# Keeping the transposed x in DRAM scratch and loading it per segment, with the gate moved into the FFN and one weight piece fewer streamed

## The chip, the cores and the metric

The kernel runs on one core of a Trainium2 chip. The metric is the device time of one execution in microseconds (us), as the median of several runs. TensorE, VectorE, ScalarE, GpSimd and SyncE are called PE, DVE, ACT, POOL and SP in the profile; PEld is a weight load of TensorE.

## The reference

Two branches see the same 2048 tokens of 640 numbers. Branch a is attention with a memory that recurs over 64 segments of 32 tokens; branch b is a gated FFN; a gate per token mixes them.

```python
g = sigmoid((x * gate_w).sum(-1, keepdims=True))
# a: 64 segments in order, 32 heads of 192; mem is 8 rows
for s in range(64):
    h = concat([mem, x[:, 32*s:32*s+32]])          # 40 rows
    q, k, v = h @ Wq, h @ Wk, h @ Wv               # 640 -> 32 x 192 each
    o = softmax(mask(q @ k.T * 192**-0.5)) @ v @ Wo
    mem = o[:, :8]; outs.append(o[:, 8:])
# b: 640 -> 1536 -> 640
b = (gelu(x @ w_gate) * (x @ w_up)) @ w_down
return g * a + (1 - g) * b                         # bf16, 2048 x 640
```

Wq, Wk, Wv and Wo are 31.5 MB together. They do not fit into SBUF, the core's working memory, and each segment needs all of them, one segment after the other.

## The kernel before

The host code lays out the program with a small scheduler: every operation names the regions that it reads and writes, and waits follow from that. The weights are cut into 84 pieces: 60 of Q, K and V (384 KB, 3072 bytes on each partition) and 24 of Wo (320 KB). What fits stays resident in SBUF; the others are streamed in every segment through a ring of five slots, spread evenly over the segment.

```python
B_RING = int(opts.get("ring", 5))
res_cap = total - wsA_total - wsB_total - ring_bytes
...
while True:                      # smallest number of streamed pieces that fits
    streamed = set()
    for k in range(nstream): ... # evenly over the time of a segment
    if tot_bytes - sum(piece_size(order[i]) for i in streamed) <= res_cap:
        break
    nstream += 1
...
def issue_ring(seg, upto):       # SP loads the next piece into the slot of five pieces ago
    slot = stream_counter[0] % B_RING
    S_.add("sp", lambda e, ...: e.dma_start(piece_view(key, ring_off[slot]), piece_src(key)),
           writes=[r_ring[slot]], dma_sem="ring%d" % slot)
```

A slot is therefore refilled only when TensorE has read it. With this layout 24 pieces are streamed (15 of Q, K, V and 9 of Wo).

First the FFN runs over all tokens and stores b in DRAM. Then the q and k of the last 8 tokens of each segment ("left", because 40 rows are 32 + 8) are computed for all segments and stored. Then come the 64 segments. Every fourth one (a group of 128 tokens) has extra work, in an order of tokens that puts the left ones last, so that rows are moved by two transfers:

```python
def perm_dma(dst, src, reads, writes, sem, watch=False):
    for i in range(2):
        S_.add(AUXQ, lambda e, i=i: e.dma_start(dst(i), src(i)), ...)   # AUXQ is ScalarE's queue
# q == 1: rows of x of the next group into rowb       (perm_dma)
# q == 3: 5 transposes of x, an eviction, 5 gate matmuls; rows of b into rowb (perm_dma)
# q == 0: mix a and b, store the output               (perm_dma)
# every segment: two GpSimd copies of x from the group's Hx into Hb
```

## Time and profile before

The median is 2167.22 us (2161.96 to 2176.56, 3 runs). From the time line, the FFN runs to 181 us, the left phase from 181 to 291 us, and the first segment then waits until 321 us for its left data. The segments follow until the end.

The page's line of engines, and the granted clock, DMA share and rate in 40 slices of the span, for the kernel before:

```profile
PE 1836.7 (85%) x40326; PEld 1154.9 (53%) x40326; DVE 1231.5 (57%) x3952; ACT 618.8 (29%) x1480; POOL 274.1 (13%) x1210
...
DMA  9203579999999999999999999999999999999998
GB/s 366 103 13 89 149 220 341 328 321 337 322 325 316 310 326 329 313 327 311 329 328 314 324 315 332 323 307 316 334 319 333 320 325 306 328 327 328 322 321 273
```

A 9 means that the DMA engines were busy 90% or more of the slice. The segments (slice 6 on, counting from 0) are 9 throughout at 306 to 341 GB/s, apart from the last slice. TensorE is busy 85%.

The windows view over 1400 us of segments gives, in order, the length, the busy time of PE, PEld, DVE, ACT and POOL with the number of instructions, then the clock, the DMA share and the rate:

```profile
500.00:1900.00 1400.00, 1188.97 (x29558) 779.79 (x29555) 878.30 (x2916) 414.44 (x1036) 204.73 (x906) 0.98 0.96 322
```

The waits view of TensorE over the same window names who waited, for what, us in total, times, longest:

```profile
PE ps L872 <- DMA arena<-in_A_Wq_dram: 58.9, 99, 1.9
PE ps L1021 <- DVE arena L1008: 27.8, 78, 0.5
PE ps L992 <- DVE arena L978: 27.6, 73, 0.7
PE ps L1021 <- DMA arena<-in_A_Wo_dram: 24.6, 46, 3.0
PE ps L899 <- DMA arena<-in_A_Wv_dram: 24.0, 41, 1.8
...
PE ps L872 <- DMA arena<-in_A_Wk_dram: 8.0, 12, 1.5
```

All waits for weight pieces come to 120 us here, 2.5 us a segment, more than all others together.

The period of a segment is read from the eviction of the new memory, once per segment on ScalarE. Its line in the view of one source line:

```profile
L1068 ACT ACTIVATE arena<-ps x63: 204/204/205, 353.1 to 2130.9; 128x40 bf16<-128x40 f32 x63
```

63 evictions from 353.1 to 2130.9 us are 62 periods of 28.67 us. A period comes from one profiled execution. The times of one kernel differ by 0.2 to 0.6% from their median, in e1 and e7 by up to 0.8%. So a difference of 0.1 to 0.2 us between two periods means nothing.

ScalarE's queue also issues the permuted transfers. This is the view of their line: duration of the issue (minimum, median, maximum, in ns) and the number.

```profile
L640 ACTq DMA_DIRECT2D arena<-in_A_x_dram x32: 647/684/1298, 0.8 to 1968.0; - x32
L640 ACTq DMA_DIRECT2D arena<-ffn_b_scratch x32: 626/638/662, 420.3 to 2143.7; - x32
L640 ACTq DMA_DIRECT2D out_dram<-arena x32: 651/653/673, 444.1 to 2163.0; - x32
```

Six such issues a group take 3.9 us of ScalarE's in-order queue.

### The profile page before, as it was taken

How to read it: one execution, taken by the hardware profiler on the slowest of the kernel's cores; microseconds unless marked ns; L12 is line 12 of the kernel's file. 1: busy time of each engine (PE TensorE's matmuls, PEld its weight loads, DVE VectorE, ACT ScalarE, POOL GpSimd, SP SyncE). 2: the span in 40 equal slices, each digit the busy share in tenths (PEclk: the TensorE clock that was granted, in tenths of full speed). 3: DMA queues.
4: the chain of work that ended last, by engine and by line, in shares of the span. 5: the costliest groups of instructions: out<-in, count | busy, mean ns of one | idle time of the engine just before them, and what ended most of it. 6: DMA issues, size and time to landing. Idle time of an engine off the chain costs nothing.

```text
span 2166.5 us, 92005 instructions
## 1 busy us (share of the span) xinstructions
PE 1836.7 (85%) x40326; PEld 1154.9 (53%) x40326; DVE 1231.5 (57%) x3952; ACT 618.8 (29%) x1480; POOL 274.1 (13%) x1210
## 2 busy tenths in 40 slices
PE   7999948888888888888888888888888888888887
PEld 3544425555555555555555555555555555555555
DVE  2222316666656566656666666656666666666665
ACT  2222212333232223332322223322323222323232
POOL 0000001111111111111111111111111111111111
PEclk9999979999999999999999999999999999999999
DMA  9203579999999999999999999999999999999998
GB/s 366 103 13 89 149 220 341 328 321 337 322 325 316 310 326 329 313 327 311 329 328 314 324 315 332 323 307 316 334 319 333 320 325 306 328 327 328 322 321 273
DMA packets 363391, 642.97 MB, mean 297 GB/s; under 512 B 60514, under 2 KB 231786, under 8 KB 362986
## 3 DMA queue, kind: packets, MB, share of 16 engines
q1 hardware_dynamic: 311914, 601.41, 81.6%
q10 hardware_dynamic: 51072, 35.66, 5.7%
q8 instruction: 315, 5.16, 0.9%
q14 instruction: 90, 0.74, 0.1%
HBM read 619.13 MB, written 17.83 MB: 294 GB/s over the span
## 4 chain that ended last, share of the span: by engine, by line
DMA 48%; PE 37%; DVE 9%; ACTq 3%; issue 2%; ACT 2%; SPq 0%; POOL 0%; DVEq 0%; POOLq 0%
DMA arena<-in_A_Wq_dram 19%; DMA arena<-in_A_Wo_dram 13%; DMA arena<-in_A_Wv_dram 10%; PE ps L872 9%; PE ps L1021 7%; PE ps L899 5%; DMA arena<-in_A_Wk_dram 4%; PE ps L804 3%; PE ps L742 2%; ACTq L819 2%; PE ps L739 2%; PE ps L757 2%; PE ps L992 2%; DVE arena L975 2%; DVE arena L1008 1%
## 5 line engine op out<-in xcount | busy, mean ns | idle before, releaser
L872 PE MATMUL ps<-arena 128*32 128x384 bf16 x10240 | 566.8, 331 | 119.9 <-DMA arena<-in_A_Wq_dram 77.6
L1021 PE MATMUL ps<-arena 128*128 128x40 bf16 x15360 | 472.1, 181 | 71.7 <-DVE arena L1008 35.9
L1021 PEld LDWEIGHTS ps<-arena 128*128 128x128 bf16 x15360 | 434.9, 97 | 116.8 <-DVE arena L1008 48.0
L872 PEld LDWEIGHTS ps<-arena 128*32 128x32 bf16 x10240 | 239.6, 96 | 346.5 <-DMA arena<-in_A_Wq_dram 172.1
L876 ACT ACTIVATE arena<-ps 128x384 bf16<-128x384 f32 x512 | 251.4, 491 | 552.2 <-PE ps L872 446.8
L899 PE MATMUL ps<-arena 128*32 128x384 bf16 x6400 | 333.1, 331 | 37.0 <-DMA arena<-in_A_Wv_dram 32.2
L835 POOL COPY arena<-arena 128x96 bf16<-128x96 bf16 x256 | 67.6, 264 | 1645.1 <-PE ps L931 1089.0
L899 PEld LDWEIGHTS ps<-arena 128*32 128x32 bf16 x6400 | 150.5, 97 | 175.6 <-DMA arena<-in_A_Wv_dram 82.0
L882 DVE STREAM_TRANSPOSE arena<-arena 128x384 bf16<-128x384 bf16 x256 | 146.0, 570 | 102.3 <-ACT arena L876 102.3
L975 DVE TENSOR_TENSOR arena<-ps,arena 128x320 bf16<-128x320 bf16 x256 | 125.8, 491 | 125.9 <-PE ps L973 121.9
L1002 ACT ACTIVATE arena<-ps 128x320 bf16<-128x320 f32 x256 | 110.7, 432 | 229.4 <-PE ps L994 229.4
L910 ACT ACTIVATE arena<-ps 128x384 bf16<-128x384 f32 x256 | 125.6, 491 | 161.9 <-PE ps L899 161.9
L839 POOL COPY arena<-arena 64x32 bf16<-64x32 bf16 (+1 forms) x768 | 165.7, 216 | 47.3
L959 DVE TENSOR_REDUCE arena<-ps 104x4 f32<-104x160 f32 x256 | 82.6, 323 | 150.6 <-ACT ps L957 148.6
L992 PE MATMUL ps<-arena 128*128 128x160 bf16 (+1 forms) x768 | 133.7, 264 | 39.6 <-DVE arena L978 38.0
L889 DVE STREAM_TRANSPOSE arena<-arena 64x128 bf16<-64x128 bf16 x512 | 145.5, 284 | 8.1
L957 ACT ACTIVATE ps<-ps 104x160 f32<-104x160 f32 x256 | 74.0, 289 | 233.9 <-DVE ps L947 189.0
L994 PE MATMUL ps<-arena 128*128 128x64 bf16 (+1 forms) x768 | 128.0, 206 | 2.1 <-DMA arena<-in_A_Wv_dram 1.0
L945 DVE TENSOR_REDUCE arena<-ps 104x4 f32<-104x160 f32 x256 | 81.0, 316 | 77.0 <-PE ps L931 77.0
L885 DVE STREAM_TRANSPOSE arena<-arena 128x256 bf16<-128x256 bf16 x256 | 111.4, 435 | 16.1 <-ACT arena L876 16.1
L992 PEld LDWEIGHTS ps<-arena 128*128 128x128 bf16 x768 | 73.9, 99 | 85.5 <-DVE arena L978 60.3
L1006 DVE CAST arena<-ps 64x160 bf16<-64x160 f32 x256 | 80.4, 314 | 52.5 <-PE ps L994 48.4
(79 smaller groups left out, 1719.8 us busy)
## 6 DMA issues: line engine op xcount, KB each, us to landing
arena<-in_A_Wo_dram SPq DMA_DIRECT2D x591, 320.0 KB, 4.9
arena<-in_A_Wq_dram SPq DMA_DIRECT2D x404, 384.0 KB, 5.3
arena<-in_A_Wv_dram SPq DMA_DIRECT2D x335, 384.0 KB, 5.1
arena<-in_A_Wk_dram SPq DMA_DIRECT2D x276, 384.0 KB, 5.3
left_qk_scratch<-arena ACTq DMA_DIRECT2D x16, 768.0 KB, 8.8
arena<-left_qk_scratch ACTq DMA_DIRECT2D x64, 192.0 KB, 4.5
arena<-in_A_x_dram SPq DMA_DIRECT2D x4, 640.0 KB, 15.1
ffn_b_scratch<-arena ACTq DMA_DIRECT2D x16, 160.0 KB, 1.8
```

Source lines behind the costliest of these rows:

```text
L839: S_.add("pool", lambda e, a=a, b=b, lo=lo, hi=hi, sa=sa: e.tensor_copy(out=Ks[lo:hi, a:b, L:R], in_=stg[lo:hi, o, 1, sa:sa + b - a]), rea ...
L872: S_.add("pe", [lambda e, j=j, k=k, gv=gv: e.matmul(ps[32 * j:32 * j + 32, bank, 0:384].rearrange("p (c i) -> p c i", i=32), Hb[hb][:, k, ...
L876: S_.add("act", lambda e: e.activation(out=rows_sb[m], in_=ps[:, bank, 0:384], func=ACTF.Copy), reads=[r_ps[bank]], writes=[r_rows[m]], na ...
L882: S_.add("dve", lambda e: e.transpose(out=Qs[:, :, 0:L], in_=rows_sb[0].rearrange("p (c r) -> p c r", r=L)), reads=[r_rows[0]], writes=[r_ ...
L885: S_.add("dve", lambda e: e.transpose(out=apx(Ks[:, 0, :], [[2 * R, 4], [R, 2], [1, L]]), in_=apx(rows_sb[1], [[96, 4], [64, 2], [1, L]])) ...
L889: S_.add("dve", lambda e, a=a, lo=lo: e.transpose(out=Ks[lo:lo + 64, a:a + 4, 0:L], in_=src[lo:lo + 64, :, 1]), reads=[r_rows[1]], writes= ...
L899: return [lambda e, j=j: e.matmul(ps[32 * j:32 * j + 32, bk, 0:384], lhs, g_[:, 384 * j:384 * (j + 1)], start=(k == 0), stop=(k == KT - 1) ...
L910: S_.add("act", lambda e: e.activation(out=v_sb[o % NVB], in_=ps[:, bank, 0:384], func=ACTF.Copy), reads=[r_ps[bank]], writes=[r_v[o % NVB ...
L975: S_.add("dve", lambda e: e.tensor_tensor(out=PTm, in0=apx(pv[:, 512:616], [[64, 2], [0, 4], [1, R]]), in1=apx(mbd, [[0, 2], [1, 4], [0, R]]),
L992: return [lambda e: e.matmul(full, v[:, e0:e0 + 128], PTm[:, ia:ib], start=True, stop=False, skip_group_check=True), lambda e: e.matmul(pa ...
L994: lambda e: e.matmul(part, vl[:, e0:e0 + 128], PTl[:, ia:ib], start=False, stop=True, skip_group_check=True)]
L1021: fns.append(lambda e, g_=g_, i=i, c=c, n=n, tl=tl, cc=cc, u=u: e.matmul(ps[:, OB, n * R:(n + 1) * R], g_[:, i, n * 128:(n + 1) * 128], u[ ...
```

## The change

The FFN transposes x anyway. The change writes that transposed x to DRAM scratch and loads 40 KB of it for each segment, so that the segments need no transposes, no copies and no second order of tokens. The gate is computed in the FFN, and b is stored already multiplied by 1 - g. The smaller buffers free 1408 bytes per partition; with what was spare before, one more piece can stay resident, and 23 are streamed. The intent is fewer weight bytes in each segment.

```diff
-    wsA["H"] = al(2 * KT * R * 2)
-    wsA["Hx"] = al(KT * 128 * 2)
-    wsA["gcol"] = al(2 * 4 * 4)
+    wsA["H"] = al(2 * KT * L * 2)
+    wsA["Hx"] = al(KT * L * 2)
+    wsA["small"] = al(NG * 4 + 8 + 32 + 16)
 ...
-    xT_sb = ....rearrange("p (k t) -> p k t", t=FB)
+    xT_sb = xT_flat.rearrange("p (s k t) -> p k s t", k=KT, t=L)   # 64-byte runs of 32 tokens
 ...
+    def gate_block(blk):            # 80 matmuls of one column, four column positions
+        ...ps[32*j : 32*j+32] <- xT_sb[:, k, sg, :], gwT[:, k:k+1], tile_position=(0, 32 * j)
-    def x_group_transposes(g, bk): ...
-    def gate_group(g, bk): ...
-    def x_copy(s): ...              # GpSimd
+    def x_load(s):                  # 128 packets of 320 bytes, from ScalarE's queue
+        aux_dma(Hb[nb]..., xts[s], ..., "xl%d" % nb)
+    def xleft_load(g):
+        aux_dma(Hx..., xls[g], ..., "xll")
 # at the end of ffn_transposes(blk):
+        aux_dma(xts[16 segments] <- xT_flat)      # 2048 packets of 320 bytes
 # ffn b evac: scale = 1 - g per row
 # segments: perm_dma (two permuted transfers) becomes aux_dma (one contiguous), no x rows, no mix1
-                    if q == 1 and g + 1 < NG:
-                        perm_dma(... rows(x2, g + 1) ...)
-                    if q == 3 and g + 1 < NG:
-                        x_group_transposes(g + 1, misc_bank())
-                        x_copy(s + 1)
+                        x_load(s + 1)
```

More of the change, by code (lines that the diff above doesn't have):

```diff
@@ L263, in _build @@
     b_scr = nc.dram_tensor("ffn_b_scratch", (S, Dm), BF, kind="Internal").ap()
+    xts = nc.dram_tensor("xt_scratch", (NSEG, 128, KT * L), BF, kind="Internal").ap()
+    xls = nc.dram_tensor("left_xt_scratch", (NG, 128, KT * L), BF, kind="Internal").ap()
     qkl = nc.dram_tensor("left_qk_scratch", (NSEG, 128, NOCT * 2 * LW), BF, kind="Internal").ap()
@@ L273, in _build @@
     wsB = {}
-    wsA["H"] = al(2 * KT * R * 2)
-    wsA["Hx"] = al(KT * 128 * 2)
-    wsA["gcol"] = al(2 * 4 * 4)
-    wsA["gwT"] = al(KT * 2)
+    wsA["H"] = al(2 * KT * L * 2)
+    wsA["Hx"] = al(KT * L * 2)
+    wsA["small"] = al(NG * 4 + 8 + 32 + 16)
     wsA["ident"] = al(128 * 2)
-    wsA["e40"] = al(R * 2)
     wsA["maskm"] = al(R * 2)
-    wsA["mbd"] = al(8)
-    wsA["mle"] = al(32)
     wsA["rowb"] = al(Dm * 2)
@@ L349, in sreg @@
         return Rg("sb", o, o + nbytes, plo, phi)
+    for k, n in (("gcol", 0), ("mbd", 4 * NG), ("mle", 4 * NG + 8), ("gwT", 4 * NG + 40)):
+        wsA_off[k] = wsA_off["small"] + n
     o_H = wsA_off["H"]
-    Hb = [bview(o_H + b * KT * R * 2, KT * R * 2).rearrange("p (k r) -> p k r", r=R) for b in range(2)]
-    r_Hm = [sreg(o_H + b * KT * R * 2, 8) for b in range(2)]
-    r_Hxp = [sreg(o_H + b * KT * R * 2 + 8, KT * R * 2 - 8) for b in range(2)]
+    Hb = [bview(o_H + b * KT * L * 2, KT * L * 2).rearrange("p (k r) -> p k r", r=L) for b in range(2)]
+    r_Hm = [sreg(o_H + b * KT * L * 2, 8) for b in range(2)]
+    r_Hxp = [sreg(o_H + b * KT * L * 2 + 8, KT * L * 2 - 8) for b in range(2)]
     o_Hx = wsA_off["Hx"]
-    Hx = bview(o_Hx, KT * 256).rearrange("p (k t) -> p k t", t=128)
-    r_Hx = sreg(o_Hx, KT * 256)
-    gcol = fview(wsA_off["gcol"], 32)
-    r_gcol = [sreg(wsA_off["gcol"] + 16 * b, 16) for b in range(2)]
+    Hx = bview(o_Hx, KT * L * 2).rearrange("p (k t) -> p k t", t=L)
+    r_Hx = sreg(o_Hx, KT * L * 2)
+    gcol = fview(wsA_off["gcol"], 4 * NG)
+    r_gcol = sreg(wsA_off["gcol"], 4 * NG)
+    gtmp = fview(o_Hx + 256, 32)
+    r_gtmp = sreg(o_Hx + 256, 32)
     gwT = bview(wsA_off["gwT"], KT * 2)
@@ L363, in _build @@
     r_ident = sreg(wsA_off["ident"], 256)
-    e40 = bview(wsA_off["e40"], R * 2)
-    r_e40 = sreg(wsA_off["e40"], R * 2)
+    e40 = ident[:, 0:R]
+    r_e40 = r_ident
     maskm = bview(wsA_off["maskm"], R * 2)
@@ L374, in _build @@
     r_rowb = sreg(wsA_off["rowb"], Dm * 2)
-    r_rowbh = [sreg(wsA_off["rowb"], Dm * 2, 0, 4 * XA), sreg(wsA_off["rowb"], Dm * 2, 4 * XA, 128)]
     Qs = bview(wsB_off["Q"], 12 * R * 2).rearrange("p (s r) -> p s r", r=R)
@@ L408, in _build @@
     r_aT4 = sreg(wsB_off["aT4"], KT * 256)
-    mem0r = bview(wsB_off["aT4"], Dm * 2)
-    r_mem0r = sreg(wsB_off["aT4"], Dm * 2)
-    gwr = bview(wsB_off["p"], 256)
-    r_gwr = sreg(wsB_off["p"], 256)
-    assert wsB_off["p"] >= ffn_off["brow"]
+    mem0r = rowb
+    r_mem0r = r_rowb
+    gwr = bview(o_Hx, 256)
+    r_gwr = sreg(o_Hx, 256)
     wg_sb = bview(ffn_off["wg"], KT * Df * 2).rearrange("p (k f) -> p k f", f=Df)
@@ L422, in _build @@
     r_xr = [sreg(ffn_off["xr"] + b * FA * Dm * 2, FA * Dm * 2) for b in range(2)]
-    xT_sb = bview(ffn_off["xT"], KT * FB * 2).rearrange("p (k t) -> p k t", t=FB)
-    r_xT = [sreg(ffn_off["xT"] + k * FB * 2, FB * 2) for k in range(KT)]
+    xT_flat = bview(ffn_off["xT"], KT * FB * 2)
+    xT_sb = xT_flat.rearrange("p (s k t) -> p k s t", k=KT, t=L)
+    r_xT = [sreg(ffn_off["xT"], KT * FB * 2)]
     gl_sb = [bview(ffn_off["gl"] + b * FB * 2, FB * 2) for b in range(2)]
@@ L434, in _build @@
     o_XL = ffn_base - XLB
-    XL = bview(o_XL, XLB).rearrange("p (k t) -> p k t", t=NL)
+    XL_flat = bview(o_XL, XLB)
+    XL = XL_flat.rearrange("p (g k t) -> p k g t", k=KT, t=L)
     r_XL = sreg(o_XL, XLB)
@@ L609, in _build @@
            reads=[r_ident], writes=[r_ident])
-    S_.add("pool", lambda e: e.memset(e40, 1.0), writes=[r_e40])
-    S_.add("pool", lambda e: e.affine_select(out=e40, in_=e40, pattern=[[-1, R]], compare_op=ALU.is_equal,
-                                             fill=0.0, base=0, channel_multiplier=1),
-           reads=[r_e40], writes=[r_e40])
     def asel(ap, reg, pattern, base, cm, fill):
@@ L630, in _build, with aux_dma @@
         S_.add("dve", lambda e, b=b: e.memset(ps[:, b, :], 0.0), writes=[r_ps[b]])
-    PP = (slice(0, 4 * XA), slice(4 * XA, 128))
-    def rows(ap, g):
-        v = ap[128 * g:128 * g + 128, :].rearrange("(s t) d -> s t d", t=L)
-        return v[:, 0:XA, :], v[:, XA:L, :]
-    def perm_dma(dst, src, reads, writes, sem, watch=False):
-        for i in range(2):
-            S_.add(AUXQ, lambda e, i=i: e.dma_start(dst(i), src(i)), reads=reads, writes=writes[i:i + 1],
-                   dma_sem="%s%d" % (sem, i), watch=watch, name=sem)
+    def aux_dma(dst, src, reads, writes, sem, watch=False):
+        S_.add(AUXQ, lambda e: e.dma_start(dst, src), reads=reads, writes=writes, dma_sem=sem, watch=watch, name=sem)
     def ffn_x_load(blk):
@@ L651, in _build @@
            writes=[r_gwr], dma_sem="gwr")
-    perm_dma(lambda i: rowb[PP[i]], lambda i: rows(x2, 0)[i], [], r_rowbh, "rowb")
     ffn_x_load(0)
@@ L658, in _build @@
     S_.add("sp", lambda e: e.dma_start(wd_sb, w_down.rearrange("(f p) n -> p f n", p=128)), writes=[r_wd], dma_sem="wd")
-    def x_group_transposes(g, bk):
-        pv = psb(bk)
-        S_.add("pe", [lambda e, k=k: e.transpose(pv[:, k * 128:(k + 1) * 128], rowb[:, k * 128:(k + 1) * 128], ident)
-                      for k in range(KT)],
-               reads=[r_rowb, r_ident], writes=[r_ps[bk]], name="xT g%d" % g)
-        S_.add("dve", lambda e: e.tensor_copy(out=Hx, in_=pv[:, 0:KT * 128].rearrange("p (k t) -> p k t", t=128)),
-               reads=[r_ps[bk]], writes=[r_Hx], name="xT evac g%d" % g)
@@ L667, in gate_group @@
-    def gate_group(g, bk):
-        b = g % 2
-        lg = ps[:, bk, 400:401]
-        S_.add("pe", [lambda e, k=k: e.matmul(lg, Hx[:, k, :], gwT[:, k:k + 1], start=(k == 0), stop=(k == KT - 1))
-                      for k in range(KT)],
-               reads=[r_Hx, r_gwT], writes=[r_ps[bk]], name="gate g%d" % g)
-        gc = gcol[:, 4 * b:4 * b + 4]
-        S_.add("act", lambda e: e.activation(out=gc[:, 2:3], in_=lg, func=ACTF.Tanh, bias=0.0, scale=0.5),
-               reads=[r_ps[bk]], writes=[r_gcol[b]], name="gate tanh g%d" % g)
-        S_.add("pool", lambda e: e.tensor_scalar(out=gc[:, 0:1], in0=gc[:, 2:3], scalar1=0.5, scalar2=0.5,
-                                                 op0=ALU.mult, op1=ALU.add),
-               reads=[r_gcol[b]], writes=[r_gcol[b]])
-        S_.add("pool", lambda e: e.tensor_scalar(out=gc[:, 1:2], in0=gc[:, 2:3], scalar1=-0.5, scalar2=0.5,
-                                                 op0=ALU.mult, op1=ALU.add),
-               reads=[r_gcol[b]], writes=[r_gcol[b]])
+    def gate_block(blk):
+        lg = ps[:, 7, 400:400 + FA]
+        fns = []
+        for k in range(KT):
+            for sg in range(FB // L):
+                j, a = sg % 4, sg // 4
+                fns.append(lambda e, k=k, sg=sg, j=j, a=a: e.matmul(
+                    lg[32 * j:32 * j + 32, a:a + 1], xT_sb[:, k, sg, :], gwT[:, k:k + 1], start=(k == 0 and a == 0),
+                    stop=(k == KT - 1), tile_position=(0, 32 * j), skip_group_check=True))
+        S_.add("pe", fns, reads=r_xT + [r_gwT], writes=[r_ps[7]], name="gate %d" % blk)
+        g4 = gcol[:, FA * blk:FA * blk + FA]
+        S_.add("act", lambda e: e.activation(out=gtmp[:, 0:FA], in_=lg, func=ACTF.Tanh, bias=0.0, scale=0.5),
+               reads=[r_ps[7]], writes=[r_gtmp], name="gate tanh")
+        S_.add("dve", lambda e: e.tensor_scalar(out=g4, in0=gtmp[:, 0:FA], scalar1=0.5, scalar2=0.5,
+                                                op0=ALU.mult, op1=ALU.add), reads=[r_gtmp], writes=[r_gcol])
+        S_.add("dve", lambda e: e.tensor_scalar(out=gtmp[:, 4:4 + FA], in0=gtmp[:, 0:FA], scalar1=-0.5, scalar2=0.5,
+                                                op0=ALU.mult, op1=ALU.add), reads=[r_gtmp], writes=[r_gtmp])
@@ L683, in chain_init, with gw_init @@
+    def gw_init():
+        pv7 = psb(7)
+        S_.add("pe", lambda e: e.transpose(pv7[:, 64:64 + KT], gwr[0:KT, :], ident[0:KT, 0:KT]),
+               reads=[r_gwr, r_ident], writes=[r_ps[7]], name="gwT")
+        S_.add("act", lambda e: e.activation(out=gwT, in_=pv7[:, 64:64 + KT], func=ACTF.Copy),
+               reads=[r_ps[7]], writes=[r_gwT], name="gwT evac")
     def chain_init():
@@ L687, in chain_init @@
                reads=[r_mem0r, r_ident], writes=[r_ps[7]], name="mem0T")
-        S_.add("pe", lambda e: e.transpose(pv7[:, 64:64 + KT], gwr[0:KT, :], ident[0:KT, 0:KT]),
-               reads=[r_gwr, r_ident], writes=[r_ps[7]], name="gwT")
+        x_load(0)
         S_.add("act", lambda e: e.activation(out=Hb[0][:, :, XA:L], in_=pv7[:, 0:KT * M].rearrange("p (k m) -> p k m", m=M),
@@ L692, in chain_init @@
                reads=[r_ps[7]], writes=[r_Hm[0]], name="mem0T evac")
-        S_.add("act", lambda e: e.activation(out=gwT, in_=pv7[:, 64:64 + KT], func=ACTF.Copy),
-               reads=[r_ps[7]], writes=[r_gwT], name="gwT evac")
-        x_group_transposes(0, 6)
-        gate_group(0, 6)
-        x_copy(0)
-    def x_copy(s):
-        nb, hx, q = s % 2, Hx, s % 4
-        S_.add("pool", [lambda e: e.tensor_copy(out=Hb[nb][:, :, 0:XA], in_=hx[:, :, q * XA:(q + 1) * XA]),
-                        lambda e: e.tensor_copy(out=Hb[nb][:, :, L:R], in_=hx[:, :, 4 * XA + q * M:4 * XA + (q + 1) * M])],
-               reads=[r_Hx], writes=[r_Hxp[nb]], name="x copy s%d" % s)
+    def x_load(s):
+        nb = s % 2
+        aux_dma(Hb[nb].rearrange("p k r -> p (k r)"), xts[s], [Rg("xt", s, s + 1)], [r_Hm[nb], r_Hxp[nb]], "xl%d" % nb)
+    def xleft_load(g):
+        aux_dma(Hx.rearrange("p k t -> p (k t)"), xls[g], [Rg("xs", g, g + 1)], [r_Hx], "xll")
     def ffn_transposes(blk):
@@ L719, in ffn_transposes @@
             eng = "dve" if bank % 2 == 0 else "act"
-            src = psb(bank)[:, 0:nk * FB].rearrange("p (k t) -> p k t", t=FB)
-            dst = xT_sb[:, k0:k0 + nk, :]
+            src = psb(bank)[:, 0:nk * FB].rearrange("p (k s t) -> p k s t", k=nk, t=L)
+            dst = xT_sb[:, k0:k0 + nk]
+            rk = [sreg(ffn_off["xT"] + 2 * k * L, 2) for k in range(k0, k0 + nk)]
             if eng == "dve":
                 S_.add("dve", lambda e, src=src, dst=dst: e.tensor_copy(out=dst, in_=src),
-                       reads=[r_ps[bank]], writes=r_xT[k0:k0 + nk])
+                       reads=[r_ps[bank]], writes=rk)
             else:
                 S_.add("act", lambda e, src=src, dst=dst: e.activation(out=dst, in_=src, func=ACTF.Copy),
-                       reads=[r_ps[bank]], writes=r_xT[k0:k0 + nk])
+                       reads=[r_ps[bank]], writes=rk)
+        ns = FB // L
+        aux_dma(xts[blk * ns:(blk + 1) * ns].rearrange("s p c -> p s c"),
+                xT_flat.rearrange("p (s c) -> p s c", c=KT * L), r_xT, [Rg("xt", blk * ns, (blk + 1) * ns)], "xts")
     def left_copy(blk):
-        ns = FB // L
-        S_.add("pool", lambda e: e.tensor_copy(
-            out=XL[:, :, blk * ns * M:(blk + 1) * ns * M].rearrange("p k (s i) -> p k s i", i=M),
-            in_=xT_sb.rearrange("p k (s t) -> p k s t", t=L)[:, :, :, XA:L]),
-            reads=r_xT, writes=[r_XL], name="XL %d" % blk)
+        gs = FB // 128
+        for a in range(gs):
+            gx = XL_flat[:, (blk * gs + a) * KT * L:(blk * gs + a + 1) * KT * L]
+            S_.add("pool", lambda e, a=a, gx=gx: e.tensor_copy(
+                out=gx.rearrange("p (k s i) -> p k s i", k=KT, i=M),
+                in_=xT_sb[:, :, 4 * a:4 * a + 4, XA:L]), reads=r_xT, writes=[r_XL], name="XL %d" % blk)
     def ffn_gu(blk):
@@ L738, in ffn_gu @@
             gb = 3 + 2 * (f % 2)
-            S_.add("pe", [lambda e, k=k, f=f, gb=gb: e.matmul(ps[:, gb, 0:FB], wg_sb[:, k, f * 128:(f + 1) * 128], xT_sb[:, k, :],
+            S_.add("pe", [lambda e, k=k, f=f, gb=gb: e.matmul(ps[:, gb, 0:FB].rearrange("p (s t) -> p s t", t=L), wg_sb[:, k, f * 128:(f + 1) * 128], xT_sb[:, k],
                                                               start=(k == 0), stop=(k == KT - 1)) for k in range(KT)],
                    reads=[r_wg] + r_xT, writes=[r_ps[gb]], name="ffn G %d %d" % (blk, f))
-            S_.add("pe", [lambda e, k=k, f=f, gb=gb: e.matmul(ps[:, gb + 1, 0:FB], wu_sb[:, k, f * 128:(f + 1) * 128], xT_sb[:, k, :],
+            S_.add("pe", [lambda e, k=k, f=f, gb=gb: e.matmul(ps[:, gb + 1, 0:FB].rearrange("p (s t) -> p s t", t=L), wu_sb[:, k, f * 128:(f + 1) * 128], xT_sb[:, k],
                                                               start=(k == 0), stop=(k == KT - 1)) for k in range(KT)],
@@ L764, in ffn_down @@
             bs = a % NBR
-            S_.add("act", lambda e, bs=bs, xb=xb: e.activation(out=brow[bs][:, 0:n1], in_=ps[:, xb, 0:n1], func=ACTF.Copy),
-                   reads=[r_ps[xb]], writes=[r_brow[bs]], name="ffn b evac")
+            S_.add("act", lambda e, bs=bs, xb=xb, a=a: e.activation(out=brow[bs][:, 0:n1], in_=ps[:, xb, 0:n1], func=ACTF.Copy,
+                                                                        scale=gtmp[:, 4 + a:5 + a]),
+                   reads=[r_ps[xb], r_gtmp], writes=[r_brow[bs]], name="ffn b evac")
             if Dm > 512:
-                S_.add("dve", lambda e, bs=bs, yb=yb: e.tensor_copy(out=brow[bs][:, 512:Dm], in_=ps[:, yb, 0:Dm - 512]),
-                       reads=[r_ps[yb]], writes=[r_brow[bs]], name="ffn b evac2")
+                S_.add("dve", lambda e, bs=bs, yb=yb, a=a: e.tensor_scalar(
+                    out=brow[bs][:, 512:Dm], in0=ps[:, yb, 0:Dm - 512], scalar1=gtmp[:, 4 + a:5 + a], scalar2=None,
+                    op0=ALU.mult), reads=[r_ps[yb], r_gtmp], writes=[r_brow[bs]], name="ffn b evac2")
             row0 = blk * FB + a * 128
@@ L779, in _build @@
         left_copy(blk)
+        if blk == 0:
+            gw_init()
+        if blk == min(1, NFB - 1):
+            chain_init()
         ffn_gu(blk)
-        if blk == 0:
-            chain_init()
+        gate_block(blk)
         if blk + 1 < NFB:
@@ L789, in _build @@
     load_residents(2)
+    for lo, hi in ((0, NG // 2), (NG // 2, NG)):
+        aux_dma(xls[lo:hi].rearrange("g p c -> p g c"),
+                XL_flat[:, lo * KT * L:hi * KT * L].rearrange("p (g c) -> p g c", c=KT * L),
+                [r_XL], [Rg("xs", lo, hi)], "xls%d" % (lo > 0))
     def kslot(i):
@@ L804, in _build @@
                 S_.add("pe", [lambda e, k=k, g_=gs[k][0], i=i, bk=bk: e.matmul(
-                    ps[:, bk, 0:NL], g_[:, i * 128:(i + 1) * 128], XL[:, k, :], start=(k == 0), stop=(k == KT - 1))
+                    ps[:, bk, 0:NL].rearrange("p (g t) -> p g t", t=L), g_[:, i * 128:(i + 1) * 128], XL[:, k], start=(k == 0), stop=(k == KT - 1))
                     for k in range(KT)], reads=[x[1] for x in gs] + [r_XL], writes=[r_ps[bk]],
@@ L846, in out_group @@
                reads=[r_aT4, r_ident], writes=[r_ps[bk]], name="aT transp g%d" % g)
-        gc = gcol[:, 4 * (g % 2):4 * (g % 2) + 4]
-        S_.add("dve", lambda e: e.tensor_scalar(out=rowb, in0=rowb, scalar1=gc[:, 1:2], scalar2=None, op0=ALU.mult),
-               reads=[r_rowb, r_gcol[g % 2]], writes=[r_rowb], name="mix1 g%d" % g)
-        S_.add("dve", lambda e: e.scalar_tensor_tensor(out=rowb, in0=pv[:, 0:Dm], scalar=gc[:, 0:1], in1=rowb,
+        S_.add("dve", lambda e: e.scalar_tensor_tensor(out=rowb, in0=pv[:, 0:Dm], scalar=gcol[:, g:g + 1], in1=rowb,
                                                        op0=ALU.mult, op1=ALU.add),
-               reads=[r_ps[bk], r_rowb, r_gcol[g % 2]], writes=[r_rowb], name="mix2 g%d" % g)
+               reads=[r_ps[bk], r_rowb, r_gcol], writes=[r_rowb], name="mix g%d" % g)
     def out_store(g):
-        perm_dma(lambda i: rows(out2, g)[i], lambda i: rowb[PP[i]], [r_rowb], [], "outw", True)
+        aux_dma(out2[128 * g:128 * g + 128, :], rowb, [r_rowb], [], "outw", True)
     OB = 7
@@ L907, in v_oct @@
             if left:
-                S_.add("pe", mms(bank2, Hx[:, k, 4 * XA:128], k, g_),
+                S_.add("pe", mms(bank2, Hx[:, k, :], k, g_),
                        reads=[rg_, r_Hx], writes=[r_ps[bank2]], name="Vl s%d o%d k%d" % (s, o, k))
@@ L1036, in segment @@
                         out_store(g - 1)
-                    if q == 1 and g + 1 < NG:
-                        perm_dma(lambda j: rowb[PP[j]], lambda j: rows(x2, g + 1)[j], [], r_rowbh, "rowb")
-                    if q == 3 and g + 1 < NG:
-                        x_group_transposes(g + 1, misc_bank())
                 if kind == "k" and i == 2:
                     if s + 1 < NSEG:
-                        x_copy(s + 1)
+                        x_load(s + 1)
                     if q == 3:
                         if g + 1 < NG:
-                            gate_group(g + 1, misc_bank())
-                        perm_dma(lambda j: rowb[PP[j]], lambda j: rows(b_scr, g)[j],
-                                 [Rg("dr", 128 * g, 128 * g + 128)], r_rowbh, "rowb")
+                            xleft_load(g + 1)
+                        aux_dma(rowb, b_scr[128 * g:128 * g + 128, :], [Rg("dr", 128 * g, 128 * g + 128)], [r_rowb], "rowb")
             elif kind == "tq":
@@ L1069, in segment @@
                    reads=[r_ps[OB]], writes=[r_Hm[nb]], name="mem evac s%d" % s)
-        S_.add("dve", lambda e: e.tensor_copy(out=aT4[:, :, q * XA:(q + 1) * XA], in_=O3[:, :, 0:XA]),
+        S_.add("dve", lambda e: e.tensor_copy(out=aT4[:, :, q * L:q * L + XA], in_=O3[:, :, 0:XA]),
                reads=[r_ps[OB]], writes=[r_aT4], name="aT evac s%d" % s)
-        S_.add("dve", lambda e: e.tensor_copy(out=aT4[:, :, 4 * XA + q * M:4 * XA + (q + 1) * M], in_=O3[:, :, L:R]),
+        S_.add("dve", lambda e: e.tensor_copy(out=aT4[:, :, q * L + XA:(q + 1) * L], in_=O3[:, :, L:R]),
                reads=[r_ps[OB]], writes=[r_aT4], name="aT evac2 s%d" % s)
+    xleft_load(0)
     stg_load(0)
```

## The prediction

> **What bounds the kernel.** The windows view gives three stages. In the first, to about 183 us, TensorE runs the FFN at 98 to 100% busy (54 to 270 us: 212 of 216 us, DMA share 0.30). From 183 to 291 us it computes the left q and k, then waits 26.7 us (295 to 321 us) for the first left-q/k load behind a full DMA queue. Then come the 64 segments, 28.7 us each (spacing of the mem evictions). There the DMA share is 0.94 to 0.96 at 315 to 322 GB/s in every window, while TensorE is busy 84%. The waits view of TensorE for 400 to 2100 us has 143 us of waits for weight pieces (2.3 us a segment) and only about 100 us for everything else. So the segments are bound by the DMA engines that stream 24 pieces of weights each; the chain of waits agrees (DMA 48%, PE 37%).
>
> **What changes, per segment.** Freed SBUF keeps one more weight piece resident: 23 are streamed instead of 24, 384 KB less. The trace's DMA records give 3072-byte packets 140 ns on average, so 128 of them over 16 engines are 1.12 us of all engines' time. Against it, x now comes as 320-byte packets: 640 a group of four segments instead of 128 of 1280 bytes (62 ns). 384-byte packets took 23.8 ns; I estimate 21 ns for 320. That is 0.84 us a group instead of 0.50, +0.09 us a segment. (The Trainium skill, "DMA: Bandwidth & Descriptors", Specifications, sets line rate at 512 bytes and above; the trace agrees mildly: 16 GB/s per engine at 384 bytes, 20.6 at 1280.) Net 1.04 us of DMA time a segment. TensorE loses ten small matmuls a group with their stalls (about 0.3 us a segment), GpSimd the x copies (0.5 us a segment), VectorE 0.84 us a group; none of these bounds.
>
> TensorE's own floor is about 23.7 busy + 1.5 us of other waits, some 25.3 us; so I take 0.95 us x 63 = 60 us.
>
> **What it costs before.** The gate becomes 80 one-column matmuls per FFN block on a bound TensorE. Today's gate matmuls are spaced about 29 ns: 2.3 us a block, 9 us in all, less 2 us for the old first transposes and gate, and partly under the wait for the last hT chunk: +6 us. The moving operand of gate, up and left matmuls gets 64-byte runs. I expect no slowdown (the skill, "SBUF — State Buffer", on 16-byte cachelines: runs of several elements in a line hit full rate); no run shows it yet. The 2048-packet x stores occupy ScalarE's queue some 2.5 us each (four left stores of that count took 10 us); hidden. No table load is added.
>
> **Prediction.** 2167 - 60 + 6 = 2113 us, range 2090 to 2145; faster by over 2%: 0.68; within 2%: 0.30; slower: 0.02.
>
> **What would show each step.** Pieces loaded: about 63 fewer; the segment period down from 28.7 by 0.95 us; DMA share still at or above 0.94; gate matmuls 2 to 3 us a block; 512-column matmuls still spaced 216 ns; x loads landing long before their segment starts.
>
> **What would make it wrong.** TensorE waits (DVE, ACT at the segment boundary) taking over as DMA slackens; small x packets slower than 21 ns or delaying piece landings; strided moving reads slowing the 512-column matmuls; a longer wait at 295 us.

## The result and the profile after

The changed kernel's median is 2103.68 us (2100.8 to 2108.07, 4 runs), against 2164.59 us for the kernel before (the three runs above and a fourth). The ratio is 0.9708, with a 95% interval of 0.9672 to 0.9744: faster by 2.9%. Here and below a ratio is the one on record for the fast runs of both kernels, which is not quite the ratio of the quoted medians (0.9719 here). The total was inside the predicted range and the direction was right.

The same views, after. First the line of engines, the DMA share and the rate on the page:

```profile
PE 1797.9 (86%) x40486; PEld 1147.2 (55%) x40486; DVE 1223.0 (58%) x3928; ACT 619.4 (29%) x1468; POOL 241.8 (12%) x1060
...
DMA  9412569999999999999999999999999999999998
GB/s 369 148 35 71 150 186 299 326 320 336 312 327 321 321 310 318 319 321 320 316 323 331 324 325 316 310 330 318 325 322 327 329 326 321 324 320 327 310 329 276
```

The windows view, 500 to 1900 us:

```profile
500.00:1900.00 1400.00, 1204.69 (x30728) 803.96 (x30720) 908.40 (x3017) 431.21 (x1068) 185.43 (x814) 1.00 0.96 322
```

The waits of TensorE in that window:

```profile
PE ps L988 <- DVE arena L974: 40.2, 94, 1.0
PE ps L1017 <- DVE arena L1004: 31.6, 91, 0.8
PE ps L895 <- DMA arena<-in_A_Wv_dram: 25.9, 35, 1.6
PE ps L868 <- DMA arena<-in_A_Wk_dram: 23.3, 42, 1.7
...
PE ps L868 <- DMA arena<-in_A_Wq_dram: 16.5, 22, 2.1
...
PE ps L1017 <- DMA arena<-in_A_Wo_dram: 10.8, 21, 1.6
```

The memory eviction:

```profile
L1059 ACT ACTIVATE arena<-ps x63: 204/204/204, 361.5 to 2069.3; 128x40 bf16<-128x40 f32 x63
```

And the issues on ScalarE's queue:

```profile
L631 ACTq DMA_DIRECT2D arena<-xt_scratch x64: 326/329/458, 62.7 to 2052.8; - x64
L631 ACTq DMA_DIRECT2D arena<-left_xt_scratch x16: 450/456/2859, 316.9 to 1968.9; - x16
L631 ACTq DMA_DIRECT2D arena<-ffn_b_scratch x16: 347/448/665, 427.2 to 2079.9; - x16
L631 ACTq DMA_DIRECT2D out_dram<-arena x16: 344/344/374, 450.2 to 2099.7; - x16
```

The period is now (2069.3 - 361.5) / 62 = 27.55 us, 1.13 us less. DMA share and rate have not moved at all. The waits for pieces fell from 120 to 77 us, 1.5 us a segment, while the two waits for VectorE rose.

The waits for pieces are not the whole gain, though. Dividing the two views by the segments in the window (1400 us over the period), TensorE's own busy time fell from 24.35 to 23.70 us a segment, its waits for pieces from 2.46 to 1.51, and its waits for VectorE and ScalarE rose from 1.59 to 2.11. The granted clock in the windows view rose from 0.98 to 1.00 with it; as an estimate from these figures, that alone is 24.35 x 0.02 = 0.5 us of the busy time. The experiments come back to this.

In three parts, the profiled span of 64.5 us less is: 8.4 us more until the first memory eviction, 70.0 us less over 62 periods, 2.9 us less after the last one.

Most of what was lost ahead of the segments goes back to one wait of TensorE in the second FFN block, in its waits view for 0 to 330 us:

```profile
PE ps L895 <- DMA arena<-left_xt_scratch: 21.6, 1, 21.6
...
PE ps L729 <- ACT arena L735: 6.3, 1, 6.3
```

The first of these lines is the wait of the first segment, which was 26.7 us before and has another name now. The second is new. Its source is seen in ScalarE's time line (start, length, instruction, idle time before it and what ended that):

```profile
46.98 0.38 ACTq L631 DMA_DIRECT2D xt_scratch<-arena  x1
49.13 0.69 ACT L755 ACTIVATE arena<-ps,arena 128x512 bf16<-128x512 f32 x1 [2.24 <-PE ps L750]
50.34 6.01 ACTq L763 DMA_DIRECT2D ffn_b_scratch<-arena  x1
...
62.66 0.46 ACTq L631 DMA_DIRECT2D arena<-xt_scratch  x1
71.28 0.20 ACT L679 ACTIVATE arena<-ps 128x40 bf16<-128x40 bf16 x1 [9.47 <-DMA arena<-xt_scratch]
71.38 1.08 ACT L735 ACTIVATE arena<-ps 128x512 bf16<-128x512 f32 x2
```

Line 679 puts the first memory into the buffer that the first x load also writes, so ScalarE waits 9.5 us for that 40 KB load. The gelu evictions (line 735) stand behind it in order, and TensorE waits 6.3 us for them to free PSUM banks, the memory that its results go to. The left phase starts 9.9 us later than before; this wait is 6.3 us of that.

The new gate, on the other hand, is cheap. The windows view around it, for its line alone (PE busy, PEld busy):

```profile
43.00:46.00 3.00, 0.77 (x80) 0.69 (x80) 1.00 1.03 402
```

### The profile page after: what moved, and what is told of

It is laid out like the page before. It is cut to its first block, busy times and chain, and to the rows that moved or that the text cites. A ratio compares the mean times of both kernels' runs of the same rounds, so it can differ in the third digit from the quotient of the medians.

```text
span 2102.0 us, 92054 instructions
## 1 busy us (share of the span) xinstructions
PE 1797.9 (86%) x40486; PEld 1147.2 (55%) x40486; DVE 1223.0 (58%) x3928; ACT 619.4 (29%) x1468; POOL 241.8 (12%) x1060
## 4 chain that ended last, share of the span: by engine, by line
DMA 39%; PE 36%; DVE 16%; ACTq 3%; ACT 3%; issue 2%; SPq 0%; DVEq 0%
DMA arena<-in_A_Wk_dram 16%; DMA arena<-in_A_Wo_dram 9%; DMA arena<-in_A_Wv_dram 8%; PE ps L1017 8%; PE ps L868 8%; PE ps L895 5%; DMA arena<-in_A_Wq_dram 5%; PE ps L803 4%; DVE arena L971 3%; PE ps L732 2%; PE ps L729 2%; ACTq L818 2%; DVE arena L1004 2%; PE ps L988 2%; DVE arena L1002 2%
## 5 line engine op out<-in xcount | busy, mean ns | idle before, releaser
L868 PE MATMUL ps<-arena 128*32 128x384 bf16 x10240 | 547.3, 329 | 95.2 <-DMA arena<-in_A_Wk_dram 32.4
L1017 PE MATMUL ps<-arena 128*128 128x40 bf16 x15360 | 457.3, 180 | 58.7 <-DVE arena L1004 38.6
L1017 PEld LDWEIGHTS ps<-arena 128*128 128x128 bf16 x15360 | 425.5, 96 | 103.3 <-DVE arena L1004 50.0
L868 PEld LDWEIGHTS ps<-arena 128*32 128x32 bf16 x10240 | 246.6, 96 | 307.2 <-DMA arena<-in_A_Wk_dram 83.8
L895 PE MATMUL ps<-arena 128*32 128x384 bf16 x6400 | 327.5, 331 | 54.0 <-DMA arena<-in_A_Wv_dram 31.5
L895 PEld LDWEIGHTS ps<-arena 128*32 128x32 bf16 x6400 | 150.9, 97 | 184.4 <-DMA arena<-in_A_Wv_dram 73.0
L988 PEld LDWEIGHTS ps<-arena 128*128 128x128 bf16 x768 | 72.7, 98 | 93.0 <-DVE arena L974 71.0
```

Source lines behind the costliest of these rows:

```text
L868: S_.add("pe", [lambda e, j=j, k=k, gv=gv: e.matmul(ps[32 * j:32 * j + 32, bank, 0:384].rearrange("p (c i) -> p c i", i=32), Hb[hb][:, k, ...
L895: return [lambda e, j=j: e.matmul(ps[32 * j:32 * j + 32, bk, 0:384], lhs, g_[:, 384 * j:384 * (j + 1)], start=(k == 0), stop=(k == KT - 1) ...
L988: return [lambda e: e.matmul(full, v[:, e0:e0 + 128], PTm[:, ia:ib], start=True, stop=False, skip_group_check=True), lambda e: e.matmul(pa ...
L1017: fns.append(lambda e, g_=g_, i=i, c=c, n=n, tl=tl, cc=cc, u=u: e.matmul(ps[:, OB, n * R:(n + 1) * R], g_[:, i, n * 128:(n + 1) * 128], u[ ...
```

## The experiments

The theory of the prediction was: the segments are bound by saturated DMA engines, so the missing piece is worth nearly its DMA time, and the work taken off the other engines is worth nothing. The first rival was that the work taken off is the gain. Twelve kernels were run. Where a piece is "read from another's place", the matmuls and their number stay the same and the result is wrong; this makes room that does not exist otherwise. Runs e1 to e4, e5 to e8, e9 to e11, and e12 were on four different chips; each ratio is to the kernel before in the same rounds.

One thing changes with every count of streamed pieces: they are spread anew over the segment. Run on its own, the kernel's selection code gives 6 of Q, 4 of K, 5 of V and 9 of Wo at 24 pieces, and 4, 6, 4 and 9 at 23. No run changes the number and keeps the places, so the worth of "a piece" below includes the new places. e5 and e6 keep both.

### e1: the change without its missing piece

```diff
-    nstream = 0
+    nstream = 24
```

> The changed kernel with its 24th piece streamed again, all else of the change kept; result right. Theory (the gain is the missing piece on a DMA-bound stage): the segment period goes back from 27.55 to about 28.7 us plus 0.1 for the small x packets, and the ratio to the kernel before is 1.00 to 1.01 (2165 to 2185 us). Rival (the gain is the work taken off TensorE, VectorE, GpSimd and ScalarE in the segments): most of the gain stays, ratio 0.97 to 0.98, period below 27.9 us.

Measured: 2148.55 us (4 runs), ratio 0.9952 (0.9894 to 1.001), period 28.26 us (its profiled execution was the fastest of the four), right result. The period meets neither side; the ratio's interval just reaches the theory's 1.00. The missing piece is worth 28.26 - 27.55 = 0.71 us a segment, not 1.1. And the rest of the change, which should have cost 0.1 us, took 0.41 us off the period (28.67 to 28.26); by the ratio, whose interval reaches 1.001, this part alone cannot be told from zero here.

### e2: the kernel before with one piece fewer

```diff
+    ALIAS = {(2, 3, 4): (2, 0, 0)}   # one V piece read from another resident one
+    nstream = 23                      # in place of 24
```

> The kernel before with one V piece fewer streamed: that piece is read from another resident V piece, so the result is wrong on purpose and nothing else changes. Theory: the period falls from 28.67 by 1.1 us and the ratio is 0.965 to 0.972. Rival: the piece is worth little by itself (ratio above 0.985).

Measured: 2117.98 us (4 runs), ratio 0.9788 (0.9752 to 0.9823), period 27.87 us. The evictions of e1 and e2, from which the periods come:

```profile
L1059 ACT ACTIVATE arena<-ps x63: 204/204/204, 358.0 to 2110.1; 128x40 bf16<-128x40 f32 x63
L1073 ACT ACTIVATE arena<-ps x63: 204/204/205, 355.4 to 2083.3; 128x40 bf16<-128x40 f32 x63
```

The piece alone gives 0.80 us a segment. The two parts can be told apart, the piece clearly, the rest by the ratio of e2 against that of the changed kernel, whose intervals just do not overlap (0.9752 against 0.9744): two ways of measuring the piece give 0.71 and 0.80 us, and two of measuring the rest give 0.41 (before against e1) and 0.32 us (e2 against the changed kernel). The ratios agree: the piece is 2.4% (e1 against the changed kernel) and 2.1% (e2), the rest 0.5% and 0.8%, of which some 8 us were lost again ahead of the segments. Neither theory was right alone. The result lies above the theory's 0.965 to 0.972.

### e3: one piece fewer still

```diff
+    ALIAS = {(2, 3, 4): (2, 0, 0)}
+    nstream = 22
```

> The changed kernel with 22 streamed pieces, one resident V piece read from another's place (wrong on purpose). If the segments are still bound by the DMA engines at 23, the period falls by another 1.05 to 1.1 us to about 26.45, and the ratio to the kernel before is 0.935 to 0.943. If TensorE or the other engines have begun to bind at 23, it falls by less than 0.7 us.

Measured: 2046.59 us (4 runs), ratio 0.9463 (0.9425 to 0.9502), period 26.74 us, that is 0.80 us less. Again it lies between the two expectations: a piece is worth about 0.7 to 0.8 us wherever it is taken.

### e4: four pieces fewer, a failed experiment

```diff
+    ALIAS = four V pieces -> (2, 0, 0)
+    nstream = 19
```

> The changed kernel with 19 streamed pieces, four V pieces read from another's place (wrong on purpose). DMA alone would give 27.55 - 4.5 = 23.1 us a segment; the TensorE floor that was predicted (busy time plus the waits that no DMA ends, 25.3 us) would stop it at about 25.0 to 25.5 us, with a DMA share near 0.86 and almost no waits for weight pieces: ratio about 0.89 to 0.90. If the period falls to 23.5 or lower, the floor was set too high; above 26, other waits take over sooner than thought.

Measured: 2329.43 us, ratio 1.0766, DMA share 0.74 and 239 GB/s from 500 to 1900 us. The kernel was misbuilt: with 19 pieces spread evenly, the piece (2, 0, 0) is itself a streamed one. By the code, four more reads a segment then go to a ring slot, wait for whatever piece is in it and hold it; in the trace TensorE waits 168 us for Wv pieces from 500 to 1900 us. It does not test the floor of TensorE. It did give the hint for the next two runs: fewer bytes, slots held longer, and a much lower rate.

### e5 and e6: four and seven slots, the same 23 pieces

```diff
# e5
-    B_RING = int(opts.get("ring", 5))
+    B_RING = int(opts.get("ring", 4))
+    nstream = 23
# e6
+    B_RING = int(opts.get("ring", 7))
+    nstream = 23;  two V pieces read from (2, 0, 0), which is resident here
```

> The changed kernel with four slots for streamed pieces instead of five, still 23 streamed pieces; result right. Theory B (bytes: the DMA engines are saturated whatever the depth): the period stays within 0.3 us of 27.55, ratio 0.970 to 0.980. Theory Q (the depth of the queue bounds: a slot is refilled only when TensorE has read it, five pieces in flight take 5 us to land, and the DMA busy share counts waiting inside the packets): the period rises by more than 1 us, ratio above 1.00.

> The changed kernel with seven slots, 23 streamed pieces, two resident V pieces read from another's place to make room (wrong on purpose). Theory B: period within 0.3 us of 27.55, ratio 0.965 to 0.972. Theory Q: the rate rises from 320 towards the 388 GB/s that the traces show at 295 to 315 us, when resident pieces are loaded without a limit on their number, and the period falls by more than 1 us, ratio below 0.94.

Measured: e5 2280.13 us (4 runs), ratio 1.0521 (1.0486 to 1.0557), right result; e6 2010.96 us (4 runs), ratio 0.9262 (0.9226 to 0.9299). The windows view of e5:

```profile
500.00:1900.00 1400.00, 1131.56 (x27925) 736.86 (x27926) 824.42 (x2738) 390.49 (x971) 167.19 (x736) 0.98 0.91 293
```

and of e6:

```profile
500.00:1900.00 1400.00, 1234.22 (x32167) 859.50 (x32164) 947.56 (x3153) 452.40 (x1117) 193.94 (x850) 1.00 0.98 337
```

The streamed bytes of a segment are the same in both and in the changed kernel; only the number of slots differs. Periods are from the memory evictions; waits for pieces are the sum of TensorE's waits for them, 500 to 1900 us, per segment; landing is the median from issue to landing of a Wk piece in the DMA view of that window.

| slots | period us | rate GB/s | DMA share | waits for pieces us | landing us |
|---|---|---|---|---|---|
| 4 (e5) | 30.32 | 293 | 0.91 | 4.0 | 4.6 |
| 5 (changed kernel) | 27.55 | 322 | 0.96 | 1.5 | 5.2 |
| 7 (e6) | 26.24 | 337 | 0.98 | 0.02 | 5.5 |

Theory B (saturated engines) falls. At the same bytes, the rate follows the number of slots, and the DMA share reads 0.91 to 0.98 in all three. In e6 TensorE waits for almost no piece any more and the share is at its highest, so the share does not say whether the DMA bounds. The supply of pieces is a closed loop: pieces per us times landing time is the number in flight. With the median landing of each kind of piece this is 23 x 5.0 / 27.55 = 4.2 of five slots in the changed kernel, 3.4 of four in e5 and 4.7 of seven in e6. Each slot that TensorE frees late is a transfer that starts late. But the engines are not free of load either: from four slots to five the pieces in flight grew by 24%, the rate by 10%, and the landing time by 13%. Depth and bytes both count (e3).

Theory Q was right about both periods and ratios. Its rate was too large for e6: expected was a rate towards 388 GB/s (the trace of the kernel before shows 376 from 295 to 315 us and 389 from 297 to 312), found was 337. With its waits for pieces gone, TensorE is then the limit. What is left of its waits in e6:

```profile
PE ps L993 <- DVE arena L979: 50.1, 116, 1.1
PE ps L1022 <- DVE arena L1009: 36.6, 98, 0.9
PE ps L873 <- ACT arena L1064: 17.6, 53, 0.4
PE ps L873 <- DVE arena L965: 15.7, 37, 1.4
...
PE ps L873 <- DMA arena<-in_A_Wk_dram: 0.6, 3, 0.3
```

(20 us of the waits are put down to "issue", which names no cause.) TensorE is busy 23.1 us of e6's period and waits 3.0 us for others, so its floor is about 26.2 us rather than the predicted 25.3.

Where a segment's time goes shows one more thing. Busy time and waits of TensorE are us a segment, from the windows and waits views, 500 to 1900 us; the clock is the mean granted clock of all runs of each kernel.

| kernel | busy | waits for pieces | waits for VectorE, ScalarE | clock |
|---|---|---|---|---|
| e5 | 24.5 | 4.0 | 1.6 | 0.966 |
| before | 24.4 | 2.5 | 1.6 | 0.981 |
| e2 | 23.9 | 1.6 | 2.3 | 0.986 |
| changed kernel | 23.7 | 1.5 | 2.1 | 0.986 |
| e3 | 23.3 | 1.0 | 2.2 | 0.990 |
| e6 | 23.1 | 0.02 | 2.6 | 0.988 |

The kernels with fewer waits for pieces ran, on the whole, at a higher granted clock and with less busy time for nearly the same matmuls. So of the 2.8 us that separate e5 from the changed kernel, 0.8 are TensorE's busy time and not waiting. And of a removed wait, part comes back as a wait for VectorE. That the waits cause the lower clock is not shown: no run sets one and leaves the other.

### e7, e8 and e9: what the rest of the change is

e7 gives the kernel before one contiguous transfer in place of each permuted pair:

```diff
-        for i in range(2):
-            S_.add(AUXQ, lambda e, i=i: e.dma_start(dst(i), src(i)), ...)
+        S_.add(AUXQ, lambda e: e.dma_start(dst, src), ...)
```

> The kernel before with one contiguous transfer in place of each permuted pair for x, b and out (tokens then in a wrong order, wrong on purpose), 24 pieces. If ScalarE's time for issuing transfers (0.65 us for each of six a group, in line before its evictions) is what the change saved besides the piece, the period falls by about 0.3 us, ratio 0.988 to 0.993. If it isn't, the ratio is 0.997 to 1.002.

e8 takes the transposes and the gate out of the kernel before:

```diff
-                    if q == 3 and g + 1 < NG:
-                        x_group_transposes(g + 1, misc_bank())
-                        if g + 1 < NG:
-                            gate_group(g + 1, misc_bank())
```

> The kernel before without the x transposes and the gate of the groups after the first (stale x and gate, wrong on purpose), 24 pieces, x still loaded. If the work taken from TensorE, VectorE and ScalarE at the end of each group is what the change saved besides the piece, the period falls by about 0.3 us, ratio 0.988 to 0.993. If the DMA bound hides it, as predicted, the ratio is 0.997 to 1.002.

Measured: e7 2141.28 us (6 runs), ratio 0.9881 (0.9848 to 0.9914), period 28.22 us; e8 2163.82 us (6 runs), ratio 0.9979 (0.9948 to 1.0009), period 28.53 us. The transposes and gate matmuls are worth nothing that can be told from zero, as predicted. The transfers are: 1.2%. In period this is 0.46 us, but e7's profiled execution was the fastest of its six, as e8's was; 1.19% of the time over 63 segments would be 0.41 us. In e7 each issue takes 0.33 us and there are three a group instead of six, so ScalarE's queue has 3.9 - 1.0 = 2.9 us a group more for its evictions. The changed kernel frees less: its seven issues a group (four of x, one each of left x, b and out) take 2.6 us by the medians above, so 1.4 us are freed, and e7's gain can't be carried over to it whole. The lines of e7:

```profile
L639 ACTq DMA_DIRECT2D arena<-in_A_x_dram x16: 339/339/393, 0.8 to 1939.1; - x16
L639 ACTq DMA_DIRECT2D arena<-ffn_b_scratch x16: 326/326/327, 418.4 to 2111.9; - x16
L639 ACTq DMA_DIRECT2D out_dram<-arena x16: 344/344/345, 442.6 to 2130.6; - x16
```

Is it ScalarE's time or the form of the transfers? e9 gives the time back:

```diff
 # e7, and after each of the three transfers:
+            for h in range(2):
+                S_.add("act", lambda e: e.activation(out=spare, in_=spare, func=ACTF.Copy), ...)
```

> The kernel of e7 (contiguous transfers, 24 pieces, wrong on purpose) with two idle-work copies of about 0.5 us on ScalarE right after each of the three transfers of a group, which give back the 2.9 us of ScalarE's time a group that e7 took away. If e7's gain is ScalarE's time, the gain goes: ratio 0.996 to 1.003. If it is the form of the transfers (rows in two permuted parts) in the DMA engines, the gain stays: ratio 0.985 to 0.991.

Measured: 2152.69 us (6 runs), ratio 0.9926 (0.9897 to 0.9954). This is between the two expectations. The two copies are 1.13 us together in the time line, 3.4 us a group, somewhat more than was taken away, and by the point estimates they give back 0.45 of the 1.19 percent. But the intervals of e7 and e9 overlap, and the chips differ. The period of 28.70 us is of no help: e9's profiled execution was the slowest of its six (2164.24 us). So it stays open how much of e7's gain is ScalarE's time and how much the form of the transfers. The trace narrows the second only a little: in the segments the 1280-byte packets of ScalarE's queue took 67.9 ns before and 57.9 in e7, which over 6016 packets and 16 engines is 0.06 us a segment.

### e10, e11 and e12: towards a better kernel

e10 issues the segment loads from SP and the FFN's x stores after those of b:

```diff
-        S_.add(AUXQ, lambda e: e.dma_start(dst, src), ...)
+        S_.add(q, lambda e: e.dma_start(dst, src), ...)     # q="sp" for x, left x and b in the segments
         ffn_down(blk)
+        if blk + 1 < NFB:
+            xt_store(blk + 1)
```

> The changed kernel with the loads of x, left x and b issued by SyncE instead of ScalarE in the segments, and the x stores of the FFN issued after the stores of b instead of before; 23 pieces, result right. The 6.3 us stall of TensorE in the second FFN block should go, and if ScalarE's issue time costs what e7 showed (0.46 us of period for 0.73 us a segment), the period falls by 0.2 to 0.35 us more: ratio 0.955 to 0.963. If ScalarE's time is not it, only the 6 us go: ratio 0.966 to 0.971.

Measured: 2097.53 us (6 runs), right, ratio 0.9676 (0.9645 to 0.9706), period 27.42 us. The move gives at most 0.3%, and the intervals of this ratio and the changed kernel's overlap; the expectation of 0.955 to 0.963 is missed, and the ratio lies in the range that was set for "ScalarE's time is not it". The move took 2.2 us of issues a group off ScalarE (by the medians of the changed kernel). But it put them in SP's queue, and the waits for pieces rose from 1.5 to 1.7 us a segment, so this does not settle e9's question. The stall in the FFN did not go: ScalarE waited for the first x load, and the store now stood right ahead of it, so that the wait of TensorE was 9.6 us.

e11 adds a sixth slot, at the price of one resident piece (24 streamed):

```diff
-    B_RING = int(opts.get("ring", 5))
+    B_RING = int(opts.get("ring", 6))
```

> As e10, with six slots, which leaves room for one resident piece fewer, so 24 are streamed; result right. A piece costs 0.7 to 0.8 us a segment (e1, e3), the sixth slot should give 0.65 us or more (e6: 1.3 us for two, e5: 2.8 us for the fifth): expected within 1.5% of e10, likely a little faster. If the bytes bound, it is slower than e10 by 2%.

Measured: 2056.84 us (6 runs), right, ratio 0.9484 (0.946 to 0.9509), period 26.97 us. More bytes and a faster kernel: the windows view has

```profile
500.00:1900.00 1400.00, 1218.93 (x31391) 824.99 (x31383) 924.99 (x3075) 438.88 (x1089) 188.14 (x828) 0.99 0.98 343
```

At 24 pieces, six slots move 343 GB/s where five moved 322 (kernel before) and 329 (e1). The change's own currency, a resident piece, is here worth less than the same 3072 bytes spent on a slot (e10 against e11).

e12 issues the x stores in the middle of the FFN blocks, and the first x load one block later:

```diff
+            if blk and f == 6:
+                xt_store(blk)
-        if blk == min(1, NFB - 1):
-            chain_init()
+        if blk == min(2, NFB - 1):
+            x_load(0)
         ffn_gu(blk)
+        if blk == min(2, NFB - 1):
+            chain_init()
```

> As e11 (six slots, 24 pieces, result right), with the x stores of FFN blocks 1 to 3 issued in the middle of their block and the first x load issued in block 2 and used after it, when the DMA queues are empty. The changed kernel had TensorE wait 6.3 us in the second FFN block because the first memory copy on ScalarE waited 9.5 us for that load; in e11 it is 9.9 us. If that is the cause, this wait goes, the segments stay at a period of 27.0 us, and the ratio to the kernel before is 0.943 to 0.946; if not, it stays at 0.948.

Measured: 2052.04 us (6 runs), right, ratio 0.9459 (0.9428 to 0.9489), period 26.97 us. In the profile the wait of TensorE for the gelu eviction, 9.9 us in e11, is gone, and the first memory eviction comes at 346.0 us instead of 358.8 us. So it is shown that the stall came from this chain of store, load and copy, though not which of the moves was needed; the gain of 0.25% in the ratio can't be told from zero, as the intervals overlap. e12 is the fastest right kernel here: 5.4% below the kernel before, while the changed kernel is 2.9% below it.

## Why the prediction was right

The total was right: 2103.7 us against 2113, 61 us less against 54. The direction follows from a step that held, that the wait for pieces was the largest wait and that one piece fewer shortens it. 63 fewer piece loads were issued, as predicted (1543 against 1606). That the number came so close is partly luck, since two steps of its sum were off and cancelled.

- **"bound by the DMA engines that stream 24 pieces": half right.** The supply of pieces is what TensorE waited for most (2.5 us a segment). That the engines were saturated was read from the share of 0.94 to 0.96, and this reading failed: e5 and e6 show that the number of slots set the rate (293, 322, 337 GB/s) with the share at 0.91 to 0.98. The check that the prediction asked for, a share still at or above 0.94, was met (0.96) and could not tell the two readings apart.
- **"Net 1.04 us of DMA time a segment", "I take 0.95 us": mis-sized.** A piece is 1.12 us of packets' time, and it was worth 0.71 us (e1), 0.80 us (e2) and 0.80 us (e3) of period. From e1 to the changed kernel the waits for pieces fell by 0.80 us a segment (2.31 to 1.51) and TensorE's busy time by 0.36, while the waits for VectorE rose by 0.42 (1.36 to 1.78).
- **"none of these bounds": wrong by 0.3 to 0.4 us a segment.** TensorE's transposes and gate are indeed worth nothing (e8). The permuted transfers on ScalarE's queue, which the prediction mentioned only as DMA time, were worth 0.4 to 0.5 us in the kernel before (e7). How much of this is ScalarE's time, and how much of it the change gets, is open (e9, e10). The rest and the piece together make the 1.13 us measured, where 0.95 was predicted.
- **Small packets: right.** The 320-byte packets took 21.3 ns on average over the execution and 22.0 in the segments (20480 in all, by the DMA records of the trace), against an estimate of 21. The Trainium skill, "DMA: Bandwidth & Descriptors", Specifications, asks for 512 bytes for line rate; here 320 bytes give 15 GB/s per engine and 1280 bytes 20.4 (62.6 ns on SP's queue).
- **"+6 us" ahead of the segments: close to the 8.4 us measured, but by luck.** The left phase starts 9.9 us later (191.4 against 181.5 us). The gate was sized at 2.3 us a block from matmuls spaced 29 ns and took 0.77 us, 9.6 ns each (3.1 us in four blocks, not 9). It uses four column positions, and the Trainium skill, "TensorE: Matmul & The Clock Gate", Part 3, says that such small tiles can run in the array at the same time; no run here tests that. The weight loads themselves are hardly shorter (93 ns each against 96 before). The x stores on ScalarE's queue, sized at 2.5 us each, took 0.38 us each to issue and were called hidden; ScalarE's wait of 9.5 us for the first x load was not foreseen: it cost TensorE 6.3 us (gone in e12).
- **Strided operands: right.** The 480 left matmuls take 104.3 us of TensorE before and after, and the 512-column FFN matmuls stay 216 ns apart, with runs of 64 bytes, as the Trainium skill, "SBUF — State Buffer", on 16-byte cachelines, lets one expect.
- **TensorE's floor: 26.2 us, not 25.3.** The waits for VectorE and ScalarE are 3.0 us once pieces are plenty (e6), not 1.5. At 23 pieces and five slots they are already 2.1 us, more than the waits for pieces.

## What to carry to other kernels

A DMA share near 1 does not prove saturated engines: multiply the transfers per us by their landing time, and if that is most of the buffers (here 4.2 of five), try one more or one fewer before counting bytes. When SBUF is scarce, compare what a buffer gives as a prefetch slot with what it gives as resident data; here six slots with 24 streamed pieces beat five with 23. And look at what the DMA issues cost the engine whose queue they stand in (here the size of that cost stayed open), and what stands behind a wait in that queue (here 6.3 us of TensorE).

## What the Trainium skill lacked or had wrong

- "DMA: Bandwidth & Descriptors", Specifications, gives an HBM limit of about 358 GB/s for a core without a condition. This core moved 366 GB/s over the first 54 us (kernel before) and 402 GB/s in a window of 3 us (changed kernel) while it loaded weights. The page does not have it wrong: further down it ties 358 to both cores of a pair streaming. For a core alone its 408.7 GB/s, under "SWDGE vs HWDGE vs iDMA", is the figure to compare with.
- No page that I used says how depth and rate go together for transfers of 320 to 384 KB. Here four, five and seven slots at equal bytes gave 293, 322 and 337 GB/s, at landing times of 4.6, 5.2 and 5.5 us.
- "Perfetto Trace Analysis", Identifying the Most-Contended Engine, does warn that the occupancy of the 16 DMA engines misleads. It has no figures; here the busy share read 0.98 while TensorE waited for almost no piece (e6), and 0.91 to 0.98 over a range of 15% in rate.
- The same DMA page lacks the time that an issue holds ScalarE's queue by the form of the transfer: 0.63 to 0.68 us for each half of a permuted pair, 0.33 to 0.46 us for one contiguous transfer of 128 rows, and 6.0 us for a b store issued 3 us after a store of 2048 packets.
- "TensorE: Matmul & The Clock Gate" has an issue floor of about 25 ns for small free dimensions (section "Back-to-back issue gap"), and about 4 ns from tile to tile for packed tiles of 512 columns (Part 3). For packed tiles of one column it has no figure: 80 one-column matmuls over 32-column weights at four column positions took 0.77 us, 9.6 ns each.
